# Building the power tables of an RWKV-5 kernel in front of its branch instead of inside it

## The chip, the cores, the metric

The kernel runs on one core of a Trainium2 chip. The metric is the device time of one execution in microseconds; medians of several executions are quoted, with the lowest and highest.

## The reference

A linear-attention block (4 batches, 8 heads, 768 steps, head size 48), then a feed-forward block without a nonlinearity in it.

```python
# attention, per step t; w and u are vectors per head
y[t]  = r[t] @ (state + (u * k[t])^T v[t])
state = w * state + k[t]^T v[t]
# bridge to 3072 x 384, then
a, b = x @ w1, x @ w2
out  = (a * b @ w3) @ w_out
```

The four weights arrive as float64 and are converted on the chip ("pieces" below).

## The kernel before

The 768 steps are cut into 6 chunks of 128; a **unit** is one chunk of one batch, so 24 units, four for each chunk. Inside a unit the decay is handled by tables of powers of w: k is multiplied by rising negative powers and r by falling ones (krs), and then all pairs of steps are one matrix product. The tables are only safe for w in [0.6, 1.6]; a flag computed from w chooses between this first path and a slower one. Everything behind the flag is inside the two arms of a branch.

```python
    # loads of w, unit 0, u, weight piece 0, unit 1, piece 1 are issued here
    nc.vector.tensor_reduce(ends[:, 0:1], wrow, AX.X, ALU.min)
    ...
    inside = nc.values_load(flag[0:1, 0:1], ...)          # the branch reads this

    def body(arm, fast):
        ...
        if fast:
            wn = tab.tile([P, LEVELS + 1, 3 * NP, 1], F32)
            nc.vector.tensor_scalar(wn[:, 0, 0:NP, :], wucol, W_LOW, W_HIGH, ALU.max, ALU.min)
            for l in range(LEVELS):                        # w^2, w^4 ...
                nc.vector.tensor_mul(wn[:, l + 1, 0:NP, :], wn[:, l, 0:NP, :], wn[:, l, 0:NP, :])
            ...                                            # reciprocals, then doubling: both
        for g, t in enumerate(natural):                    # 8 transposes, 2 copies: pn
            ...
        def scale(n):
            kr = krin[n % NIN]
            nc.vector.tensor_mul(krs[n % NS][:, :, :, :D], kr, pn[:, :, :, :D])   # krs
            nc.vector.tensor_mul(ruk, kr[:, 0], kr[:, 1])                         # bonus with u
            nc.vector.tensor_mul(ruk, ruk, ub)
            nc.vector.tensor_reduce(dg, ruk, AX.X, ALU.add)
            # 8 diagonals of AT on ScalarE
        def turn(n):   # krs transposed on TensorE, copied out by ScalarE: kT, rT
        def pairs(n):  # kT x rT on TensorE; VectorE copies the upper triangle into AT
        def output(n): # AT x v on TensorE, copied to xT by ScalarE
        def update(n): # new state: TensorE, then VectorE
        def convert(piece, raw):   # float64 to float32: one pass of ScalarE, six of VectorE
```

Behind this, chunk c's attention runs beside the feed-forward products of chunk c-1 and the conversion of weights. Six pieces (each 128x512; three of w1 and three of w2) must be converted before the first products ps_a and ps_b of the feed-forward part can be finished. The program states what depends on what; the order in each engine's queue is chosen by the scheduler when the kernel is built.

Of the kernel before, what the change touches and what calls it, by code (L numbers as in the profile page):

```python
# [8 lines left out]
F32 = mybir.dt.float32  # L9
# [3 lines left out]
ALU = mybir.AluOpType  # L13
# [3 lines left out]
PSUM = bass.MemoryType.PSUM  # L17
# [3 lines left out]
def kernel(  # L21
# [27 lines left out]
    nc = tc.nc  # L49
    B, H, S, D = r.shape  # L50
    P = 128
    C = 128
    HC = C // 2
    NCH = S // C
    PAD = 64
    NP = H // 2
# [5 lines left out]
    LEVELS = 7  # L62
    PIECE = 512
    W_LOW, W_HIGH = 0.6, 1.6
# [3 lines left out]
    const = ctx.enter_context(tc.tile_pool(name="const", bufs=1))  # L68
# [5 lines left out]
    ident = const.tile([P, P], F32)  # L74
# [13 lines left out]
    wucol = const.tile([P, NP, 1], F32)  # L88
# [46 lines left out]
    for i in range(2):  # L135
# [3 lines left out]
                      in_=u.rearrange("h d -> (h d)").rearrange("(o n) -> o n", o=1).to_broadcast([P, DM]))  # L139
# [8 lines left out]
    nc.vector.tensor_reduce(ends[:, 1:2], wrow, AX.X, ALU.max)  # L148
    nc.vector.tensor_scalar(ends[:, 2:3], ends[:, 0:1], W_LOW, None, ALU.is_ge)
    nc.vector.scalar_tensor_tensor(flag, ends[:, 1:2], W_HIGH, ends[:, 2:3], ALU.is_le, ALU.mult)  # L150
    inside = nc.values_load(flag[0:1, 0:1], min_val=0, max_val=1,
                            skip_runtime_bounds_check_because="a comparison's result is 0 or 1")

    def program(fast):
        with ExitStack() as arm:
            body(arm, fast)

    def body(arm, fast):
        tab = arm.enter_context(tc.tile_pool(name="tab", bufs=1))
        work = arm.enter_context(tc.tile_pool(name="work", bufs=2))  # L160
        psT = arm.enter_context(tc.tile_pool(name="psT", bufs=2, space=PSUM))
# [5 lines left out]
        for t in st:  # L167
            nc.gpsimd.memset(t, 0.0)
        if fast:

            wn = tab.tile([P, LEVELS + 1, 3 * NP, 1], F32)
            nc.vector.tensor_scalar(wn[:, 0, 0:NP, :], wucol, W_LOW, W_HIGH, ALU.max, ALU.min)
            for l in range(LEVELS):
                nc.vector.tensor_mul(wn[:, l + 1, 0:NP, :], wn[:, l, 0:NP, :], wn[:, l, 0:NP, :])  # L174
            nc.vector.reciprocal(wn[:, 0:LEVELS, NP:2 * NP, :], wn[:, 0:LEVELS, 0:NP, :])
            nc.vector.tensor_copy(out=wn[:, 0:LEVELS, 2 * NP:, :], in_=wn[:, 0:LEVELS, 0:NP, :])

            both = tab.tile([P, 2, NP, C], F32)
            nc.vector.memset(both[:, 0, :, HC:HC + 1], 1.0)
            nc.vector.tensor_copy(out=both[:, 1, :, HC:HC + 1], in_=wn[:, 0, NP:2 * NP, :])  # L180
            bf = both.rearrange("x g p t -> x (g p) t")
            for l in range(LEVELS):
                n = 1 << l
                if n < HC:
                    nc.vector.tensor_mul(bf[:, :, HC + n:HC + 2 * n], bf[:, :, HC:HC + n],
                                         wn[:, l, NP:, :].to_broadcast([P, 2 * NP, n]))
                nc.vector.tensor_mul(bf[:, :, HC - 2 * n + 1:HC - n + 1] if n < HC else bf[:, :, 0:1],
                                     bf[:, :, HC - n + 1:HC + 1] if n < HC else bf[:, :, HC:HC + 1],
                                     wn[:, l, 0:2 * NP, :].to_broadcast([P, 2 * NP, n if n < HC else 1]))
            natural = [both[:, g] for g in range(2)]  # L190
        else:
            wn = tab.tile([P, LEVELS + 1, NP, 1], F32)
            nc.vector.tensor_copy(out=wn[:, 0], in_=wucol)
            pw = tab.tile([P, NP, C], F32)
            pr = tab.tile([P, NP, C], F32)
            nc.vector.memset(pw[:, :, 0:1], 1.0)
            nc.vector.memset(pr[:, :, C - 1:C], 1.0)
            for l in range(LEVELS):
                n = 1 << l
                by = wn[:, l].to_broadcast([P, NP, n])  # L200
                nc.vector.tensor_mul(pw[:, :, n:2 * n], pw[:, :, 0:n], by)
                nc.vector.tensor_mul(pr[:, :, C - 2 * n:C - n], pr[:, :, C - n:C], by)
                nc.vector.tensor_mul(wn[:, l + 1], wn[:, l], wn[:, l])
            natural = [pr]
        wc = wn[:, LEVELS, 0:NP, :]
        pn = tab.tile([C, len(natural), H, PAD], F32)
        for g, t in enumerate(natural):
            ps = psT.tile([P, NP, C], F32, tag="t", name=f"ps_p{g}")
            for p in range(NP):
                nc.tensor.transpose(ps[:, p, :], t[:, p, :], ident)  # L210
            nc.scalar.copy(out=pn[:, g].rearrange("t h d -> t (h d)"), in_=ps.rearrange("x p t -> x (p t)"))


        def convert(piece, raw):
# [238 lines left out]
        for c in range(NCH):  # L453
            done = 0
            for b in range(B):
                n = c * B + b
# [52 lines left out]
```

## Time and profile before

| | before |
|---|---|
| time, median of 4 (lowest to highest) | 569.03 us (568.66 to 569.62) |
| span of the profiled execution | 567.8 us |
| TensorE busy / VectorE / ScalarE | 534.4 / 254.9 / 169.2 us |
| VectorE busy in the first 60 us | 46.99 us |
| first transposes of the tables; first krs | 21.46 us; 24.08 us |

How to read the profile: the page's rows of digits cut the span into 40 slices and give an engine's busy share in tenths. The table of stretches gives each engine's busy time (and instructions, in brackets) in a stretch. The timeline lists instructions in order of time: start, duration, engine, line, operation, output <- input, size, count, and in square brackets how long the engine was idle before and what released it. In an engine's list of waits the columns are: who waited, for whom, total us, how many times, the longest. The prediction below shows these lines for the kernel before.

### The profile page before, as it was taken

What the parts mean: (1) busy time and instruction counts of PE and PEld (TensorE: products, weight loads), DVE (VectorE), ACT (ScalarE), POOL (GpSimd) and SP (SyncE); (2) the same over time, 40 slices, a digit from 0 to 9 for tenths busy, and PEclk for the clock granted to TensorE, in tenths of its full rate; (3) what the DMA queues carried; (4) which work ended last, traced back from release to release, by engine and by line L of the source; (5) the groups of instructions that cost most, each with busy time, mean ns of one, the idle gap of its engine ahead of it and who ended that gap; (6) DMA issues with size and microseconds to landing.
All of it is one profiled execution on the core that took longest, in us unless ns stands there. A gap on an engine that the chain in (4) does not pass through costs nothing.

```text
span 567.8 us, 8077 instructions
## 1 busy us (share of the span) xinstructions
PE 534.4 (94%) x3304; PEld 304.8 (54%) x3304; DVE 254.9 (45%) x495; ACT 169.2 (30%) x400; POOL 3.5 (1%) x17
## 2 busy tenths in 40 slices
PE   0388999999999999999999999999999999999996
PEld 0266554555655575566645555655555555544453
DVE  2899999999584596760030404133111100001100
ACT  1555454444333353431121212132132110111010
POOL 2000000000000000000000000000000000000000
PEclk9999999999999999999999999999999999999998
DMA  7675553445233243220120202021010000000001
GB/s 151 171 171 142 132 147 108 128 143 154 43 102 104 87 116 89 66 43 14 43 43 1 65 18 57 15 56 29 16 28 7 9 15 14 29 28 0 0 16 46
DMA packets 84129, 37.52 MB, mean 66 GB/s; under 512 B 76273, under 2 KB 79474, under 8 KB 84082
## 3 DMA queue, kind: packets, MB, share of 16 engines
q1 hardware_dynamic: 84082, 36.91, 25.0%
q8 instruction: 28, 0.46, 0.3%
q14 instruction: 19, 0.16, 0.1%
HBM read 32.18 MB, written 4.72 MB: 65 GB/s over the span
## 4 chain that ended last, share of the span: by engine, by line
PE 87%; DVE 7%; SPq 2%; issue 1%; ACT 1%; DMA 1%; ACTq 0%; DVEq 0%
PE ps_o L406 22%; PE ps_b L400 21%; PE ps_a L395 20%; PE ps_w L259 7%; PE ps_a L299 4%; PE ps_y L355 3%; PE ps_y L347 3%; PE ps_kT L287 2%; PE ps_s L373 2%; PE ps_rT L287 1%; PE ps_w3T L255 1%; SPq L109 1%; DMA krin<-in_r_dram 1%; DVE krs L269 1%; DVE AT L302 1%
## 5 line engine op out<-in xcount | busy, mean ns | idle before, releaser
L401 DVE TENSOR_TENSOR abt<-ps_b,a 128x512 f32<-128x512 f32 x48 | 33.2, 691 | 223.1 <-PE ps_b L400 197.7
L395 PE MATMUL ps_a<-xT,w 128*128 128x512 f32 x288 | 133.2, 597 | 0.0
L400 PE MATMUL ps_b<-xT,w 128*128 128x512 f32 x288 | 132.1, 593 | 0.1
L406 PE MATMUL ps_o<-w,abt 128*128 128x384 f32 x384 | 127.2, 488 | 0.0
L406 PEld LDWEIGHTS ps_o<-w,abt 128*128 128x128 f32 x384 | 72.0, 190 | 49.2 <-issue 2.0
L400 PEld LDWEIGHTS ps_b<-xT,w 128*128 128x128 f32 x288 | 54.4, 190 | 68.9 <-issue 64.3
L395 PEld LDWEIGHTS ps_a<-xT,w 128*128 128x128 f32 x288 | 53.1, 190 | 56.6 <-issue 50.9
L281 ACT ACTIVATE AT<-ident,dg 128x128 f32<-128x128 f32 x192 | 59.1, 391 | 5.8 <-DVE wn L174 3.2
L397 ACT COPY a<-ps_a 128x512 f32<-128x512 f32 x48 | 28.1, 585 | 106.0 <-PE ps_a L395 105.8
L302 DVE COPY_PREDICATED AT<-later,ps_a 128x512 f32<-128x512 int32 x48 | 32.9, 731 | 30.7 <-PE ps_a L299 30.3
L409 ACT COPY osb<-ps_o 128x384 f32<-128x384 f32 x24 | 11.5, 479 | 108.7 <-PE ps_o L406 85.7
L259 PE MATMUL ps_w<-wo,w3T 128*128 128x384 f32 x128 | 43.1, 490 | 0.2 <-ACT w3T L256 0.2
L223 ACT ACTIVATE power<-raw 128x512 f32<-128x512 f32 (+1 forms) x36 | 23.6, 655 | 38.6 <-DVE t L230 23.7
L299 PEld LDWEIGHTS ps_a<-rT,kT 64*128 64x128 f32 x384 | 25.4, 190 | 16.4 <-issue 9.4
L359 ACT COPY xT<-ps_y 128x384 f32<-128x384 f32 x24 | 11.4, 476 | 73.7 <-PE ps_y L355 73.5
L259 PEld LDWEIGHTS ps_w<-wo,w3T 128*128 128x128 f32 x128 | 23.7, 190 | 15.9 <-ACT w3T L256 1.0
L299 PE MATMUL ps_a<-rT,kT 64*128 64x128 f32 x384 | 30.7, 289 | 1.2 <-ACT rT L290 0.8
L355 PE MATMUL ps_y<-AT,vnat 128*32 128x128 f32 x768 | 28.3, 274 | 2.9 <-DVE AT L302 1.5
L290 ACT COPY kT<-ps_kT 128x512 f32<-128x512 f32 x24 | 14.1, 587 | 36.6 <-PE ps_kT L287 36.5
L355 PEld LDWEIGHTS ps_y<-AT,vnat 128*32 128x32 f32 x768 | 22.4, 110 | 4.5 <-DVE AT L302 2.5
L230 DVE SCALAR_TENSOR_TENSOR t<-raw,power 128x512 f32<-128x512 uint32 (+1 forms) x36 | 23.7, 658 | 0.2
L269 DVE TENSOR_TENSOR krs<-krin,pn 128x768 f32<-128x768 f32 x24 | 22.9, 957 | 0.6
(64 smaller groups left out, 335.3 us busy)
## 6 DMA issues: line engine op xcount, KB each, us to landing
raw<-in_moe_w_dram SPq DMA_DIRECT2D x28, 512.0 KB, 3.8
krin<-in_k_dram SPq DMA_DIRECT2D x24, 192.0 KB, 2.7
krin<-in_r_dram SPq DMA_DIRECT2D x24, 192.0 KB, 3.4
vnat<-in_v_dram SPq DMA_DIRECT2D x24, 192.0 KB, 2.8
out_dram<-osb SPq DMA_DIRECT2D x24, 192.0 KB, 1.9
raw<-in_moe_w_out_dram SPq DMA_DIRECT2D x8, 384.0 KB, 3.0
ub<-in_u_dram SPq DMA_DIRECT2D x1, 192.0 KB, 5.3
wucol<-in_w_dram SPq DMA_DIRECT2D x2, 0.8 KB, 1.8
```

The source lines that it names most:

```text
L230: nc.vector.scalar_tensor_tensor(t, lo, 2.0 ** -52, power, ALU.mult, ALU.mult)
L259: nc.tensor.matmul(ps, lhsT=w3T[:, kc, :], rhs=wo[kc], start=(kc == 0), stop=(kc == KF - 1))
L269: nc.vector.tensor_mul(krs[n % NS][:, :, :, :D], kr, pn[:, :, :, :D])
L281: nc.scalar.activation(out=AT[n][:, i, p, :], in_=ident, func=COPY, scale=dg[:, h:h + 1])
L299: nc.tensor.matmul(ps[i][:, p, :], lhsT=kT[n][rows(i), p, :], rhs=rT[n][rows(i), p, :], start=True, stop=True)
L302: nc.vector.copy_predicated(AT[n][:, i], later.bitcast(I32)[:, None, :].to_broadcast([C, NP, C]), ps[i])
L355: nc.tensor.matmul(to(q, g), lhsT=vv[:, p, x:x + Q], rhs=AT[n][:, i, p, :], start=(not c and m < P // Q), stop=True, skip_group_check=True)
L395: nc.tensor.matmul(pa, lhsT=w1[:, q, js], rhs=xT[c][:, q, :], start=(q == 0), stop=(q == KM - 1))
L397: nc.scalar.copy(out=a, in_=pa)
L400: nc.tensor.matmul(pb, lhsT=w2[:, q, js], rhs=xT[c][:, q, :], start=(q == 0), stop=(q == KM - 1))
L401: nc.vector.tensor_mul(abt[c, j], pb, a)
L406: nc.tensor.matmul(po, lhsT=abt[c, j][:, b * C:(b + 1) * C], rhs=w34[:, j, :], start=(j == 0), stop=(j == KF - 1))
```

## The change

The intent: the tables need only w, which lands early, yet in the kernel before their instructions mix in VectorE's queue with work that waits for the first units. Put in front of the branch, they can't be interleaved with anything inside it.

```diff
+    pn_in = const.tile([C, 2, H, PAD], F32)
+    with tc.tile_pool(name="once", bufs=1) as once, tc.tile_pool(name="psW", bufs=2, space=PSUM) as psW:
+        wn_in = const.tile([P, LEVELS + 1, 3 * NP, 1], F32)
+        nc.vector.tensor_scalar(wn_in[:, 0, 0:NP, :], wucol, W_LOW, W_HIGH, ALU.max, ALU.min)
+        ...  # the same squarings, reciprocals and doublings, into wn_in and both
+        for g in range(2):
+            ps = psW.tile([P, NP, C], F32, tag="w", name=f"ps_p{g}")
+            for p in range(NP):
+                nc.tensor.transpose(ps[:, p, :], both[:, g, p, :], ident)
+            nc.scalar.copy(out=pn_in[:, g].rearrange("t h d -> t (h d)"), in_=ps.rearrange("x p t -> x (p t)"))
     inside = nc.values_load(flag[0:1, 0:1], ...)
@@ inside the branch
         if fast:
-            wn = tab.tile(...)   # and all of the above
+            wc, pn = wn_in[:, LEVELS, 0:NP, :], pn_in
```

More of the change, by code (lines that the diff above doesn't have):

```diff
@@ L150 @@
     nc.vector.scalar_tensor_tensor(flag, ends[:, 1:2], W_HIGH, ends[:, 2:3], ALU.is_le, ALU.mult)
+    pn_in = const.tile([C, 2, H, PAD], F32)
+    with tc.tile_pool(name="once", bufs=1) as once, tc.tile_pool(name="psW", bufs=2, space=PSUM) as psW:
+        wn_in = const.tile([P, LEVELS + 1, 3 * NP, 1], F32)
+        nc.vector.tensor_scalar(wn_in[:, 0, 0:NP, :], wucol, W_LOW, W_HIGH, ALU.max, ALU.min)
+        for l in range(LEVELS):
+            nc.vector.tensor_mul(wn_in[:, l + 1, 0:NP, :], wn_in[:, l, 0:NP, :], wn_in[:, l, 0:NP, :])
+        nc.vector.reciprocal(wn_in[:, 0:LEVELS, NP:2 * NP, :], wn_in[:, 0:LEVELS, 0:NP, :])
+        nc.vector.tensor_copy(out=wn_in[:, 0:LEVELS, 2 * NP:, :], in_=wn_in[:, 0:LEVELS, 0:NP, :])
+        both = once.tile([P, 2, NP, C], F32)
+        nc.vector.memset(both[:, 0, :, HC:HC + 1], 1.0)
+        nc.vector.tensor_copy(out=both[:, 1, :, HC:HC + 1], in_=wn_in[:, 0, NP:2 * NP, :])
+        bf = both.rearrange("x g p t -> x (g p) t")
+        for l in range(LEVELS):
+            n = 1 << l
+            if n < HC:
+                nc.vector.tensor_mul(bf[:, :, HC + n:HC + 2 * n], bf[:, :, HC:HC + n],
+                                     wn_in[:, l, NP:, :].to_broadcast([P, 2 * NP, n]))
+            nc.vector.tensor_mul(bf[:, :, HC - 2 * n + 1:HC - n + 1] if n < HC else bf[:, :, 0:1],
+                                 bf[:, :, HC - n + 1:HC + 1] if n < HC else bf[:, :, HC:HC + 1],
+                                 wn_in[:, l, 0:2 * NP, :].to_broadcast([P, 2 * NP, n if n < HC else 1]))
+        for g in range(2):
[3 more added lines that the diff above has]
+            nc.scalar.copy(out=pn_in[:, g].rearrange("t h d -> t (h d)"), in_=ps.rearrange("x p t -> x (p t)"))
     inside = nc.values_load(flag[0:1, 0:1], min_val=0, max_val=1,
@@ L169, in body @@
         if fast:
-            wn = tab.tile([P, LEVELS + 1, 3 * NP, 1], F32)
-            nc.vector.tensor_scalar(wn[:, 0, 0:NP, :], wucol, W_LOW, W_HIGH, ALU.max, ALU.min)
-            for l in range(LEVELS):
-                nc.vector.tensor_mul(wn[:, l + 1, 0:NP, :], wn[:, l, 0:NP, :], wn[:, l, 0:NP, :])
-            nc.vector.reciprocal(wn[:, 0:LEVELS, NP:2 * NP, :], wn[:, 0:LEVELS, 0:NP, :])
-            nc.vector.tensor_copy(out=wn[:, 0:LEVELS, 2 * NP:, :], in_=wn[:, 0:LEVELS, 0:NP, :])
-            both = tab.tile([P, 2, NP, C], F32)
-            nc.vector.memset(both[:, 0, :, HC:HC + 1], 1.0)
-            nc.vector.tensor_copy(out=both[:, 1, :, HC:HC + 1], in_=wn[:, 0, NP:2 * NP, :])
-            bf = both.rearrange("x g p t -> x (g p) t")
-            for l in range(LEVELS):
-                n = 1 << l
-                if n < HC:
-                    nc.vector.tensor_mul(bf[:, :, HC + n:HC + 2 * n], bf[:, :, HC:HC + n],
-                                         wn[:, l, NP:, :].to_broadcast([P, 2 * NP, n]))
-                nc.vector.tensor_mul(bf[:, :, HC - 2 * n + 1:HC - n + 1] if n < HC else bf[:, :, 0:1],
-                                     bf[:, :, HC - n + 1:HC + 1] if n < HC else bf[:, :, HC:HC + 1],
-                                     wn[:, l, 0:2 * NP, :].to_broadcast([P, 2 * NP, n if n < HC else 1]))
-            natural = [both[:, g] for g in range(2)]
+            wc, pn = wn_in[:, LEVELS, 0:NP, :], pn_in
         else:
@@ L203, in body @@
                 nc.vector.tensor_mul(wn[:, l + 1], wn[:, l], wn[:, l])
-            natural = [pr]
-        wc = wn[:, LEVELS, 0:NP, :]
-        pn = tab.tile([C, len(natural), H, PAD], F32)
-        for g, t in enumerate(natural):
-            ps = psT.tile([P, NP, C], F32, tag="t", name=f"ps_p{g}")
+            wc = wn[:, LEVELS]
+            pn = tab.tile([C, 1, H, PAD], F32)
+            ps = psT.tile([P, NP, C], F32, tag="t", name="ps_pr")
             for p in range(NP):
-                nc.tensor.transpose(ps[:, p, :], t[:, p, :], ident)
-            nc.scalar.copy(out=pn[:, g].rearrange("t h d -> t (h d)"), in_=ps.rearrange("x p t -> x (p t)"))
+                nc.tensor.transpose(ps[:, p, :], pr[:, p, :], ident)
+            nc.scalar.copy(out=pn[:, 0].rearrange("t h d -> t (h d)"), in_=ps.rearrange("x p t -> x (p t)"))
         def convert(piece, raw):
```

## The prediction

> **What bounds the kernel now.** I read the page first, then the stretch table, the list of waits by stretch, and the timeline of VectorE for the first 60 us. The page says TensorE, and the last digits of its row say where it does not.
>
> ```profile
> PE 534.4 (94%) x3304; PEld 304.8 (54%) x3304; DVE 254.9 (45%) x495; ACT 169.2 (30%) x400; POOL 3.5 (1%) x17
> PE   0388999999999999999999999999999999999996
> DVE  2899999999584596760030404133111100001100
> ```
>
> A slice is 14.2 us. TensorE is idle in the first slice, a third busy in the second, and full from the fifth. VectorE is the reverse: 45% over the whole, but full from the second to the tenth slice. So the kernel has a head, where VectorE sets the pace, and a long body, where TensorE does. The table of stretches (columns: stretch, its length, busy time and instructions of TensorE, its weight loads, VectorE, ScalarE, GpSimd, then clock, DMA share, GB/s) puts the border near 60 us:
>
> ```profile
> 12.00:18.00 6.00, 0.00 (x0) 0.00 (x0) 4.24 (x17) 2.83 (x11) 0.00 (x0) 1.00 1.04 234
> 18.00:24.00 6.00, 1.94 (x8) 1.57 (x8) 6.00 (x21) 3.69 (x10) 0.00 (x0) 1.00 0.36 111
> 30.00:45.00 15.00, 12.20 (x211) 9.47 (x209) 14.85 (x30) 9.95 (x27) 0.00 (x0) 1.00 0.63 151
> 45.00:60.00 15.00, 13.26 (x175) 9.69 (x176) 14.81 (x28) 7.66 (x21) 0.00 (x0) 1.00 0.64 150
> 60.00:75.00 15.00, 15.00 (x121) 8.17 (x120) 14.82 (x30) 7.81 (x21) 0.00 (x0) 1.00 0.59 157
> ```
>
> From 60 us the list of TensorE's waits shows 0.4 us in all up to the end. An improvement of the head therefore reaches the end nearly whole, and nothing else does. Now the head, from VectorE's timeline (start, duration, engine, line, operation, and in brackets the idle time in front of it and its releaser):
>
> ```profile
> 3.21 0.15 DVE L150 SCALAR_TENSOR_TENSOR flag<-ends 1x1 int32<-1x1 f32 x1
> 4.22 0.28 DVE L172 TENSOR_SCALAR wn<-wucol 128x4 f32<-128x4 f32 x1 [0.86 <-DMA wucol<-in_w_dram]
> 6.24 0.56 DVE L274 TENSOR_TENSOR ruk<-krin 128x384 f32<-128x384 f32 x1 [1.74 <-DMA krin<-in_r_dram]
> 6.72 0.16 DVE L174 TENSOR_TENSOR wn<-wn 128x4 f32<-128x4 f32 x1
> 12.96 0.56 DVE L274 TENSOR_TENSOR ruk<-krin 128x384 f32<-128x384 f32 x1 [6.09 <-DMA krin<-in_r_dram]
> 13.44 0.15 DVE L174 TENSOR_TENSOR wn<-wn 128x4 f32<-128x4 f32 x1
> ...
> 17.89 0.56 DVE L274 TENSOR_TENSOR ruk<-krin 128x384 f32<-128x384 f32 x1 [0.80 <-DMA krin<-in_r_dram]
> ...
> 20.92 0.42 DVE L187 TENSOR_TENSOR both<-both,wn 128x256 f32<-128x256 f32 x1
> ...
> 24.08 1.83 DVE L269 TENSOR_TENSOR krs<-krin,pn 128x768 f32<-128x768 f32 x2
> ```
>
> The order in VectorE's queue mixes the tables (wn, both) with the bonus product ruk of the next units. Its data were on chip at 4.22, but the second squaring stands behind the ruk of unit 1, which waits 6.09 us for a transfer, and the last table stands behind the ruk of unit 2. So TensorE gets the tables at 21.46, pn is in SBUF at 24.05, and the first krs (scaled k and r of unit 0) starts at 24.08. Only then can any pair product run.
>
> [...] GpSimd's first memset behind the branch starts at 4.06, 0.70 us after the flag ends at 3.36. [...] 76273 of 84129 packets are under 512 B, and the engines are 1.04 busy at only 234 GB/s in 12 to 18 us. Hence no krin comes earlier by this change before 18 us.
>
> **The change part by part.** Removed from the branch and put in front of it: 25 VectorE instructions, 8 transposes, 2 ScalarE copies. No arithmetic is added or dropped, no shape changes. The sum of work is the same; what moves is time.
>
> Table time. Interleaved as they are now, the tables' start-to-start distances sum to 3.2 us (first clamp 0.22, memset 0.06, seven squarings 0.07 each, reciprocal 0.24, two copies 0.2, thirteen table products 0.40+0.21+1.34 = 1.95). Alone they run in a dependent chain. The flag's chain shows such a pair: L149 at 3.05, L150 at 3.21, so 0.16 per small step in place of 0.07: seven squarings cost 0.6 more, and about 0.4 more for reciprocal, copy and the first products. So 4.2 us, from 4.22 to **8.4**. From the first transpose to pn it is 24.05 − 21.46 = 2.6 us now; the same behind 8.4 gives pn at **11.1**. That is 13 us earlier than 24.05.
>
> That is not the gain, because VectorE sets the pace of the head and its work stays. From 24 to 135 us its list of waits has one entry, 0.9 us. What can be won is idle time of VectorE. Now it idles 0.87+1.17+0.86+1.74+6.09+0.80+0.91 = **12.4 us** up to 28.3. After the change I count: 0.87+1.17+0.86 as before (nothing lands sooner); 1.0 latency inside the chain of tables; 0.7 for its branch, now behind the tables, which takes it to 9.1; ruk of unit 0 to 9.6. Then the order decides. If the ruk of unit 1 still stands in front of the first krs, 12.96 − 9.6 = 3.3 idle; together 7.9. If krs of unit 0 comes first, about 2.0 from 9.1 to 11.1; together 6.6. Behind that there is enough to do up to the landing of unit 2 at 17.89: two krs 1.8, the ruk and dg of two units 2.8, the first converted weight piece 3.1, AT of unit 0 1.3, together 9.0 against 4.9 to 6.8 us. So the gain is 12.4 − 7.9 = 4.5 or 12.4 − 6.6 = 5.8, less a lost 0 to 1 for a wait on ScalarE or a raw piece. I choose 5.0, and 568.8 − 5.0 = **563.8 us**.
>
> **The rivals.**
> (1) The whole 13 us come through, 556 us. For it: TensorE's first real work, krs, is the last link before all else, and 13 us is what its input gains. Against it: VectorE is at 14.85 of 15 in 30 to 45 us, and the first two-weight product of the second part, ps_b at 59.85, comes with the sixth converted piece (its last addition ends at about 60). It can't come earlier than VectorE's work allows.
> (2) A transfer takes the place of the wait, gain 0 to 2 us, 567 to 569. For it: DMA is full from 4.5 to 18 us, so units 1 and 2 land at 12.96 and 17.89 whatever VectorE does, and an earlier VectorE runs into them. Against it: its share is 0.36 in 18 to 24 and 0.63 later, and the loads that follow wait for buffers that VectorE would free sooner (the krin load at 25.07 starts as the first krs ends).
> (3) The order of the whole branch is laid out anew, since its start differs; a few us either way, at TensorE's border above all. Neither trace nor source shows its size.
> (4) ScalarE or TensorE becomes late because each now passes its branch only behind the tables (about 11 us). Against it: raw of piece 0 lands at 11.41 and TensorE has nothing before krs. I give it under 1 us.
>
> **Range and chances.** Rival 2 gives the upper end, 567.5; a good order with half of rival 1 the lower end, 558.5. Faster by over 2% needs 557.4, a gain of 11.4 of the 12.4 us that VectorE idles, hence 0.06. Slower by over 2% would need 11.4 us of new waits in a body that has none: 0.01. The rest, 0.93, is within 2%.
>
> **What would show it.** In the changed kernel: last table product at about 8.4 and first transpose just behind it; pn at about 11; first krs at 11 to 15; VectorE's idle time up to 28 us at 7 to 8 instead of 12.4; VectorE near full from 18 us on; TensorE without waits from about 55 us instead of 60; busy sums of all engines unchanged within 1%. I am wrong if the order puts krs behind the ruk of unit 2 again (krs after 18 us), if TensorE's waits between 60 us and the end grow past 2 us, or if VectorE turns out not to pace the head, so that the gain follows krs.

Sentences of the prediction on the hardware in general, which no trace of this case shows, are cut, and the cuts are marked. Its sum came to 568.8 − 5.0 = 563.8 us, and the 0.7 us for the branch is taken from the trace (the flag ends at 3.36, GpSimd's first memset starts at 4.06). What it calls a full DMA from 4.5 to 18 us is a mean share of 0.96 in the table of stretches.

## The result

| | before | after |
|---|---|---|
| time, median of 4 | 569.03 us | 565.00 us (564.53 to 565.27) |
| span of the profiled execution | 567.8 us | 562.7 us |
| mean granted clock of TensorE | 0.997 | 0.989 |
| VectorE busy in the first 60 us | 46.99 us | 51.54 us |
| first transposes of the tables; first krs | 21.46; 24.08 us | 8.00; 10.65 us |

The ratio is 0.9927 (95% interval 0.991 to 0.9945). Ratios here are the mean time of one kernel's fast runs over that of the other's of the same rounds, so not quite the ratio of the medians. The change is clearly real and clearly under 2%.

The rows of digits of the changed kernel, for TensorE, VectorE and the granted clock:

```profile
PE   3869999999999999999999999999999999999996
DVE  5999999998674696840220414233211100001100
PEclk9969999999999999999999999999999999999999
```

VectorE is full one slice sooner and done sooner. TensorE starts earlier but is no better in its third slice (6), and its clock falls there, which it did not before. VectorE's timeline of the changed kernel, same columns as in the prediction:

```profile
3.57 0.17 DVE L157 TENSOR_SCALAR wn_in<-wucol 128x4 f32<-128x4 f32 x1 [0.22 <-DMA wucol<-in_w_dram]
...
3.78 1.34 DVE L159 TENSOR_TENSOR wn_in<-wn_in 128x4 f32<-128x4 f32 x7
...
7.43 0.42 DVE L172 TENSOR_TENSOR both<-both,wn_in 128x256 f32<-128x256 f32 x1
10.65 0.96 DVE L277 TENSOR_TENSOR krs<-krin,pn_in 128x768 f32<-128x768 f32 x1 [2.80 <-ACT pn_in L179]
...
12.57 0.96 DVE L277 TENSOR_TENSOR krs<-krin,pn_in 128x768 f32<-128x768 f32 x1 [0.50 <-DMA krin<-in_r_dram]
...
17.45 0.56 DVE L282 TENSOR_TENSOR ruk<-krin 128x384 f32<-128x384 f32 x1 [0.65 <-DMA krin<-in_r_dram]
17.92 1.34 DVE L310 COPY_PREDICATED AT<-later,ps_a 128x512 f32<-128x512 int32 x2
```

The squarings now run back to back, 1.34 us for seven. The tables end at 7.85, and VectorE waits 2.80 us for pn. The first krs stands in front of the products of unit 1 and starts 13.43 us earlier than before. AT of unit 0 is made at 17.92, before at 29.75: 11.8 us earlier. And yet the end came only 4 to 5 us earlier. Where the other 8 us went can be followed unit by unit: the second half of AT ends at 31.1, 34.3, 41.7, 46.3, 55.6, 62.9 us for units 0 to 5 before, and at 19.3, 25.4, 30.0, 41.6, 50.4, 58.6 after. The lead is 11.8, 8.9, 11.7, and from unit 3 on 4.7, 5.2, 4.3 us.

What ends the lead at unit 3 are two things beside VectorE. First, ScalarE's queue in the changed kernel has the eight diagonals between its two copies of unit 3 (its timeline):

```profile
34.62 0.59 ACT L298 COPY kT<-ps_kT 128x512 f32<-128x512 f32 x1 [2.45 <-PE ps_kT L295]
35.10 2.45 ACT L289 ACTIVATE AT<-ident,dg 128x128 f32<-128x128 f32 x8
37.45 0.56 ACT L298 COPY rT<-ps_rT 128x512 f32<-128x512 f32 x1
```

so TensorE waits 2.7 us for rT. Second, TensorE's clock. The table of stretches for three short stretches of the changed kernel (the number behind GpSimd's brackets is the granted clock):

```profile
28.00:30.00 2.00, 0.79 (x13) 0.40 (x11) 2.00 (x5) 1.35 (x4) 0.00 (x0) 1.00 0.38 75
30.00:32.00 2.00, 1.42 (x34) 1.15 (x36) 1.94 (x5) 0.88 (x2) 0.00 (x0) 0.87 0.37 83
34.00:36.00 2.00, 1.38 (x7) 0.98 (x5) 1.91 (x6) 1.38 (x5) 0.00 (x0) 0.50 1.05 196
```

After 2.2 us of work in 4 us, with idle times of 1.02, 0.19 and 0.58 us between, the clock was 0.50 from 32 to 41 us (0.65 from 41 to 42, then 1.00). In the same rows VectorE is busy 2.00, 1.94 and 1.91 of 2 us. That is the question for the experiments: did the stall at unit 3 and the half clock eat the lead (**theory B**), or was it never there to be had, because VectorE had no time to use it (**theory A**, that of the prediction)?

### The profile page after: what moved, and what is told of

The parts are those of the page before. It is cut to its first block, busy times and chain, and to the rows that moved or that the text cites. A ratio compares the mean times of both kernels' runs of the same rounds, so it can differ in the third digit from the quotient of the medians.

```text
span 562.7 us, 8088 instructions
## 1 busy us (share of the span) xinstructions
PE 539.0 (96%) x3304; PEld 307.2 (55%) x3304; DVE 255.5 (45%) x495; ACT 169.2 (30%) x400; POOL 3.6 (1%) x17
## 4 chain that ended last, share of the span: by engine, by line
PE 90%; DVE 6%; DMA 1%; issue 1%; ACT 1%; SPq 0%; DVEq 0%; ACTq 0%
PE ps_o L414 22%; PE ps_b L408 22%; PE ps_a L403 22%; PE ps_w L267 7%; PE ps_a L307 5%; PE ps_y L363 4%; PE ps_y L355 3%; PE ps_kT L295 2%; PE ps_s L381 2%; PE ps_rT L295 2%; PE ps_w3T L263 1%; DVE t L238 1%; DVE AT L310 1%; DMA raw<-in_moe_w_dram 1%; DVE w L239 1%
## 5 line engine op out<-in xcount | busy, mean ns | idle before, releaser
L277 DVE TENSOR_TENSOR krs<-krin,pn_in 128x768 f32<-128x768 f32 x24 | 22.9, 956 | 3.8 <-ACT pn_in L179 2.8
```

## The experiments

Twelve kernels were run, in three groups, each group on one chip with the kernel before beside it. They are told in the order of the argument, so 12 and 11 stand before 10. Times are medians; "against after" compares with 565.00 us, and ratios with 0.9927.

**1. The tables stay inside the branch, but go first.** Every later instruction of VectorE in the branch was queued behind the tables:

```diff
 kernel before, inside body()
-                nc.vector.tensor_mul(bf[...], bf[...], wn[...])
+                last = nc.vector.tensor_mul(bf[...], bf[...], wn[...])
...
+        queue.enter_context(tc.issue_after(last.ins))     # around all units
         scale(0)
```

> The kernel before, with the tables left inside the branch, but every other instruction of VectorE in the branch queued behind the squarings and copies of the tables. Theory A (VectorE paces the head, the gain is the idle time it loses): the tables end near 9 us, VectorE then waits for unit 1 until about 12.9 us, and its idle time up to 30 us falls from 12.4 to about 7 us; time about 564 us, as good as the change, although the first krs comes at about 16 us, 5 us later than in the changed kernel. Theory B (the moment of the first krs sets the gain): krs at 16 us is 8 us earlier than before against 13.4 us in the changed kernel, so the gain is about 60% of 4.0 us, about 566.5 us. Theory C (the place in front of the branch is what counts): no gain, 569 us.

Measured: 563.87 us (563.51 to 564.49), ratio 0.9906 (0.9891 to 0.992). VectorE's timeline of this kernel:

```profile
4.34 0.28 DVE L172 TENSOR_SCALAR wn<-wucol 128x4 f32<-128x4 f32 x1 [0.86 <-DVE flag L150]
...
9.99 0.56 DVE L276 TENSOR_TENSOR ruk<-ruk,ub 128x384 f32<-128x384 f32 x1 [2.34 <-DMA ub<-in_u_dram]
...
15.84 1.82 DVE L270 TENSOR_TENSOR krs<-krin,pn 128x768 f32<-128x768 f32 x2
```

The edge had been hung on the last product in program order, which depends on little and runs early, so ruk of unit 0 still slipped into the tables and met a wait of 2.34 us for u. The first krs came at 15.84, 5.2 us later than in the changed kernel. The time was as good all the same, and so was VectorE's idle time up to 28 us: 6.5 us, against 6.75 in the changed kernel. (The clock stayed at 0.996 to 0.999 here, against 0.989; experiment 9 comes back to what that is worth.) So the moment of krs does not set the gain (against B's 566.5), and the place in front of the branch is not needed for it (against C's 569): the order is.

**2 and 3. Spare work for VectorE behind the tables, in front of the branch.** Three and ten products of 128x512 that nobody reads; the order in the branch stays that of the changed kernel (compared for the first hundred instructions of VectorE).

```diff
 changed kernel, behind the tables
+        for _ in range(3):                                # or 10
+            nc.vector.tensor_mul(spare, both[:, 0], both[:, 1])
```

> The changed kernel with three products of 128x512 (about 1.8 us of VectorE) put behind the last table product in front of the branch, read by nobody. They fall into the 2.8 us in which VectorE waits for pn. Theory A: nothing is lost, 565 us within 0.6. If instead all added work of VectorE costs its full length: 566.8 us.

> The changed kernel with ten such products (about 6.0 us of VectorE), same order in the branch. 2.1 to 2.8 us of it lie in the wait for pn, the rest delays VectorE. Theory A: the rest, 3.2 to 3.9 us, comes out at the end one for one: about 568.5 us. Theory B (latency of the units through TensorE and ScalarE limits): krs moves from 10.65 to about 14 us, and since 13.4 us of krs gave 4.0 us, 3.5 us of krs give about 1 us: 566 us.

Measured: with three, 565.08 us (563.95 to 567.57), ratio 0.9927 (0.9909 to 0.9945), the same as the changed kernel. With ten, 568.20 us (567.21 to 568.34), ratio 0.9973 (0.996 to 0.9986). VectorE's timeline with ten:

```profile
7.89 7.23 DVE L177 TENSOR_TENSOR spare<-both 128x512 f32<-128x512 f32 x10
15.32 0.96 DVE L280 TENSOR_TENSOR krs<-krin,pn_in 128x768 f32<-128x768 f32 x1 [0.20 <-DMA raw<-in_moe_w_dram]
```

They cost 0.72 us each, not the 0.6 I had taken (in the kernel before, a 128x512 product starts at 22.32 and the next instruction at 22.93), so 7.2 us in all; 2.8 lie in the wait for pn, and krs comes 4.67 us later. The time grew by 3.2 us, not by the 4.4 that are left: the changed kernel's two waits for transfers, 0.50 and 0.65 us, are gone in this run, which makes up the difference. The expected 568.5 was met although the size of a product behind it was not. Here krs is at 15.32, about where experiment 1 has it (15.84), and the times differ by 4.3 us. The same first krs, another time: what differs is how much of VectorE's time before it was work. Theory A holds for both; B, which gives the two the same time, falls.

**4. The bonus products of units 0 to 5 on GpSimd.**

```diff
-            nc.vector.tensor_mul(ruk, kr[:, 0], kr[:, 1])
-            nc.vector.tensor_mul(ruk, ruk, ub)
+            eng = nc.gpsimd if n < 6 else nc.vector
+            eng.tensor_mul(ruk, kr[:, 0], kr[:, 1])
+            eng.tensor_mul(ruk, ruk, ub)
```

> The changed kernel with the two products for the bonus (ruk) of units 0 to 5 on GpSimd in place of VectorE, which takes 6 x 0.94 = 5.6 us of work off VectorE in the head. Theory A: VectorE reaches the border about 5 us earlier and the end follows, about 560 us, provided that GpSimd keeps up and the two don't slow each other. Theory B (ScalarE's late copy of rT for unit 3 and the low clock of TensorE there set the end): within 1 us of 565 us.

Measured: 570.59 us (569.25 to 571.07), ratio 1.0016 (1.0003 to 1.0029): both theories missed. GpSimd and VectorE did slow each other. The timelines of VectorE and of GpSimd in this kernel:

```profile
13.36 1.49 DVE L232 SCALAR_TENSOR_TENSOR w<-power,raw 128x512 f32<-128x512 f32 x1
14.88 1.10 DVE L234 TENSOR_SCALAR t<-w 128x512 uint32<-128x512 uint32 x1
...
17.31 0.68 DVE L232 SCALAR_TENSOR_TENSOR w<-power,raw 128x512 f32<-128x512 f32 x1
```

```profile
12.52 1.78 POOL L283 TENSOR_TENSOR ruk<-krin 128x384 f32<-128x384 f32 x1 [1.48 <-DMA krin<-in_r_dram]
14.26 2.57 POOL L284 TENSOR_TENSOR ruk<-ruk,ub 128x384 f32<-128x384 f32 x2
```

The same conversion step took 1.49 us while GpSimd worked and 0.68 us after it had stopped; the plain bitwise step 1.10 against 0.41. GpSimd's first product for a unit took 1.78 us at 12.52, beside VectorE's krs, and 1.00 us at 23.61. Not every instruction was slowed: the reduction dg took its usual 0.53 us at 28.37, beside a product on GpSimd. The run does not test A, since VectorE got no time back (126.35 us of work up to 135 us, against 125.80 in the changed kernel, with twelve products fewer). Nor is this slowing alone to blame: the order changed as well, the first reductions dg came at 22.98 instead of 14.39, and AT of unit 0 at 27.14 instead of 17.92.

**5. The stall at unit 3 taken away.** ScalarE copies rT before it makes the diagonals, units 0 to 5.

```diff
-            # diagonals of AT in scale(n)
+            # ... in turn(n), queued behind the copy of rT
+                with tc.issue_after(copied.ins):
+                    diagonals(n, owed.pop(n))
```

> The changed kernel with ScalarE's copy of rT queued ahead of the eight diagonals of the same unit, for units 0 to 5; this takes away TensorE's wait of 2.7 us for rT of unit 3 and should spare it the low clock between 31 and 41 us. Work of VectorE the same. Theory A (VectorE paces the head): within 1 us of 565. Theory B (that wait and the low clock ate most of the 13 us): 3 to 5 us faster, about 561.

Measured: 564.61 us (563.76 to 564.71), ratio 0.9915 (0.9901 to 0.9928). The wait for rT fell from 2.7 to 0.8 us, and the time did not follow. But TensorE did not stop waiting; it now stands in front of ps_y of unit 3:

```profile
38.23 1.33 DVE L321 COPY_PREDICATED AT<-later,ps_a 128x512 f32<-128x512 int32 x2
39.05 0.64 PE L374 MATMUL ps_y<-AT,vnat 128*32 128x128 f32 x4 [3.97 <-issue]
```

VectorE, busy without a gap from 35.19 us on, came to AT of unit 3 only at 38.23; the profile names no releaser, but TensorE goes on as the first half of AT ends (about 38.9). TensorE's waits behind the tables add to 10.4 us up to 60 us, against 10.0 in the changed kernel. So the stall was moved rather than taken away, from ScalarE's copy to VectorE's; that speaks for A, and the first half of theory B falls. The clock still fell (0.78 from 30 to 45 us, 0.992 on the mean), so the other half stays for experiment 9.

**6. Less work for VectorE.** No product with u for units 0 to 5, no last addition for the first six pieces; relative error 0.31. Its output is wrong, which doesn't matter for the time.

```diff
+            if n >= 6:
                 nc.vector.tensor_mul(ruk, ruk, ub)
...
+            if not any(src is p[1] for p in ab_pieces[:6]):
                 nc.vector.tensor_add(dst, dst, t)
```

> The changed kernel with less work for VectorE in the head and nothing put in its place: no product with u for units 0 to 5 (6 x 0.47 us) and no last addition for the first six weight pieces (6 x 0.6 us), 6.4 us in all. The result is wrong on purpose. Theory A: up to 6.4 us faster, about 559; less where VectorE then runs into transfers or into TensorE. Theory B: no more than 1 us faster.

Measured: 560.99 us (558.91 to 561.82), ratio 0.9849 (0.9829 to 0.9868): 4.0 us of 6.4 against after. More than B allows, less than one for one. VectorE's waits for ps_a and for a krin grew from 0.7 and 0.6 to 1.5 and 1.4 us, but in all it idled only 1.1 us more of the first 60 us (9.6 against 8.5). That leaves about 1.3 us of the missing 2.4 unexplained. With 6 us less to do, VectorE seems no longer alone in setting the pace.

**7. The first states on ScalarE.**

```diff
-                    nc.vector.tensor_mul(own, ps[rows(i), :, 0:D], wc[rows(i)].to_broadcast([PAD, NP, D]))
+                    for p in range(NP):
+                        nc.scalar.activation(out=own[:, p, :], in_=ps[rows(i), p, 0:D], func=COPY, scale=wc[rows(i), p, :])
```

> The changed kernel with the first state of each batch (two products of 0.35 us each, four units) written by ScalarE, eight small scaled copies a unit, in place of VectorE; correct. VectorE loses 2.8 us of work in the head, ScalarE, which is half idle there, gains some 6 us. Theory A: 1.5 to 3 us faster than 565, about 562.5. Theory B (ScalarE's queue limits): slower than 565.

Measured: 561.47 us (559.47 to 563.03), ratio 0.9862 (0.9841 to 0.9884), correct: 3.5 us against after, the fastest correct kernel. More than the 2.8 us of work moved (ScalarE's eight copies took 1.73 to 1.75 us a unit, 7.0 in all where some 6 were expected), and its runs scatter by 3.6 us. Its clock was 0.995 to 1.0, against 0.989 in the changed kernel, so a part may be the clock's. Experiments 10 and 11 show that the size does not carry over.

**8. Spare work for VectorE behind the border**, twelve products of 128x384 at units 8 and 9.

```diff
+            if n in (8, 9):
+                for _ in range(6):
+                    nc.vector.tensor_mul(ruk, kr[:, 0], kr[:, 1])
```

> The changed kernel with twelve more products of 128x384 on VectorE for units 8 and 9, 5.6 us of work at about 95 to 110 us, where VectorE is still full but TensorE has no waits. If TensorE sets the pace from about 60 us on: within 1 us of 565. If VectorE, being full up to 135 us, paces that stretch too: about 570.

Measured: 566.32 us (565.59 to 567.90), ratio 0.9944 (0.993 to 0.9957): 1.3 us against after (the intervals overlap), not the 5.6. The products ran from 90.7 to 105.4 us; from 90 to 105 us VectorE was busy 14.86 of 15 us. TensorE's waits behind 60 us stayed at 0.9 us. So VectorE may be full without setting the pace; from 60 us on it has a backlog that TensorE does not wait for. Even the 1.3 us need not come from them: in the profiled run, the slowest of the five at 567.90 us, the clock had already fallen to half at 20 us, in a head whose order is that of the changed kernel.

```profile
20.00:24.00 4.00, 4.00 (x52) 3.08 (x50) 1.93 (x5) 1.81 (x5) 0.00 (x0) 0.50 0.78 208
```

In that stretch VectorE worked 1.93 of 4 us, against 3.43 in the changed kernel. It waited 2.1 us for TensorE there, for ps_s; a second wait for ps_s at 49 us brings this to 3.2 us.

**9. Spare transposes that hold the clock**, 64 of them, in TensorE's gaps between 23 and 47 us.

```diff
+        def filler(n, k, behind):                         # behind update(n) and turn(n), units 0 to 3
+            with tc.issue_after(behind.ins):
+                ps = psF.tile([P, KF // 2, P], F32, tag="f", ...)
+                for q in range(k):
+                    nc.tensor.transpose(ps[:, q % (KF // 2), :], ident, ident)
```

> The changed kernel with spare transposes on TensorE (8 to 20 of 128x128 per unit, 60 in all, into a bank that nothing reads) in its gaps between 20 and 45 us, so that its clock is not lowered there. VectorE's work is the same. If VectorE alone paces the head: within 1 us of 565. If the half clock from 31 to 41 us cost part of the gain: 2 to 3 us faster, about 562.5, and with less scatter between runs.

Measured: 563.83 us (563.26 to 565.63), ratio 0.991 (0.9895 to 0.9925). The recorded clock held (0.996 to 1.0 in all five runs). The medians differ by 1.2 us, and the interval overlaps that of the changed kernel. So from 23 us on, the low clock did not eat the 8 us of lead. What it cost in all stays open, because the spare transposes start only at 23.0 us. Before them TensorE came late in this profiled run (the slowest of the five), although the table of stretches gives a clock of 1.00 from 12 to 30 us: from the start of AT of unit 0 to that of the state which needs ps_s there were 4.77 us (18.37 to 23.14), in the changed kernel 3.13 (17.92 to 21.05), and VectorE waited for ps_s:

```profile
23.14 0.82 DVE L399 TENSOR_TENSOR st<-ps_s,wn_in 64x192 f32<-64x192 f32 x2 [2.07 <-PE ps_s L390]
```

So a late TensorE acts through VectorE's waits, here (2.07 us) and in experiment 8 (2.1 us). Among the kernels with the changed order the two slowest runs, 567.57 us in experiment 2 and 567.90 us in experiment 8, are the two with the lowest clock, 0.981, while their siblings at 0.989 to 0.993 took 563.95 to 566.37 us. The prediction of less scatter did not hold (2.4 us).

**12. The wait for pn filled with work that has to be done anyway**: piece 0 is loaded first and converted behind the tables, in front of the branch.

```diff
-    load(0)
-    ...
-    landed = {0: fetch(ab_pieces[0])}
+    landed = {0: fetch(ab_pieces[0])}
+    load(0)
...
+        nc.scalar.activation(out=power0, in_=hi.bitcast(F32), func=ABS)
+        with tc.issue_after(table.ins):
+            ...   # the six VectorE passes of convert() for piece 0
```

> The changed kernel with the first weight piece loaded ahead of unit 0 and converted in front of the branch behind the tables, so that VectorE works (3.3 us) while TensorE and ScalarE make pn, where it waited 2.8 us. No work is added or dropped. Theory A: the wait of 2.8 us goes, the first krs comes about 1 us later (11.8), the time falls by about 2 us to 563. Theory B (latency of the first units): about 1 us slower than 565.

Measured: 562.83 us (561.74 to 563.66), ratio 0.9888 (0.9871 to 0.9905), correct: 2.2 us faster than after, as A said, with the first krs 1.1 us later (the six passes ran from 7.76 to 11.54, 3.8 us where 3.3 were expected):

```profile
10.85 0.69 DVE L187 TENSOR_TENSOR w<-w,t 128x512 f32<-128x512 f32 x1
11.75 0.96 DVE L290 TENSOR_TENSOR krs<-krin,pn_in 128x768 f32<-128x768 f32 x1 [0.20 <-DVE w L187]
```

The size is partly luck. The 2.80 us are gone, but new waits for TensorE, 1.8 and 1.1 us, took most of that back: VectorE idled 5.8 us up to 28 us, against 6.75. The rest came from 30 to 60 us (0.4 us idle against 1.3), where the clock was less low (0.89 from 30 to 45 us, against 0.66); on the mean it was 0.996 to 0.999, and experiment 9, with such a clock and nothing moved, is only 1.0 us slower than this one, with overlapping intervals. The direction is plain, together with experiment 3: useful work in the gap did not lengthen the kernel, useless work beyond the gap did, and krs is delayed by both.

**11. The first states on ScalarE, in the kernel before.** The edit is that of experiment 7.

> The kernel before with the first states on ScalarE (2.8 us less for VectorE in the head), as in the run of the changed kernel where this brought 3.5 us. Theory A: the same here, 2 to 3.5 us faster than before, about 566.

Measured: 569.53 us (568.99 to 570.67), ratio 1.0012 (0.9998 to 1.0026): nothing, against theory A. The table of stretches suggests why:

```profile
30.00:45.00 15.00, 12.94 (x197) 9.76 (x198) 13.76 (x26) 12.73 (x42) 0.00 (x0) 0.89 0.63 151
45.00:60.00 15.00, 13.07 (x190) 9.44 (x188) 14.59 (x28) 14.88 (x50) 0.00 (x0) 1.00 0.70 162
```

ScalarE is busy 14.88 of 15 us from 45 to 60, and VectorE is no longer full from 30 to 45. The states of units 0 to 3 (1.75 us of ScalarE each) fall together with the diagonals, the copies and the conversions there; in the changed kernel the same work came from 21 to 39 us, and ScalarE had 6.26 of 15 us to do from 45 to 60. So it looks as if VectorE's time can be cashed in only where ScalarE has room; no run tests this.

**10. All that had helped, together**: experiments 7, 9 and 12.

> All that theory A says should help, put together: the changed kernel, the first piece converted in the wait for pn (2 us), the first states on ScalarE (3 us), spare transposes that keep the clock (0 to 2 us): 558 to 560 us, correct.

Measured: 563.13 us (562.22 to 563.70), ratio 0.9892 (0.9877 to 0.9908), correct. No better than experiment 12 alone. VectorE was busy 53.92 us of the first 60, as wanted, but the first product of the feed-forward part came at 50.77 us, in experiment 12 at 43.38. TensorE was busy 14.42 of 15 us from 30 to 45, so it had few gaps left for the spare transposes; I take it that these now cost what they saved, but no run without them was made, and the loss stays open.

## Why the prediction was right

It said 563.8 us (558.5 to 567.5), within 2%; measured 565.00.

**That VectorE paces the head: shown, within limits.** Two lines of the table of stretches, for the first 60 us, of the kernel before and of the changed one:

```profile
0.00:60.00 60.00, 32.22 (x423) 24.87 (x424) 46.99 (x110) 28.46 (x73) 3.54 (x17) 1.00 0.67 157
```

```profile
0.00:60.00 60.00, 41.92 (x458) 29.44 (x458) 51.54 (x118) 30.84 (x78) 3.58 (x17) 0.91 0.72 169
```

VectorE got 4.55 us more done in the first 60 us, and the span shrank by 5.1 us. TensorE's busy time there grew by 9.7 us, part of it at half clock, and bought nothing more. The same count for every kernel that has the same work to do before the border (spare products taken off, span of the same execution):

| kernel | VectorE's useful work in 60 us | span | sum |
|---|---|---|---|
| before | 46.99 | 567.8 | 614.8 |
| 3, ten spare products | 54.86 − 7.23 = 47.63 | 566.5 | 614.1 |
| 8, late spare products | 48.05 | 566.1 | 614.2 |
| 9, spare transposes | 50.41 | 563.8 | 614.2 |
| 2, three spare products | 52.67 − 2.14 = 50.53 | 563.7 | 614.2 |
| after | 51.54 | 562.7 | 614.2 |
| 5, rT first | 51.75 | 562.6 | 614.4 |
| 1, order only | 52.66 | 561.7 | 614.4 |
| 12, piece 0 in the gap | 53.38 | 561.2 | 614.6 |

Work gained and span lost agree within 0.5 us about their mean. This table alone says only how far VectorE had come by 60 us, not who held it up: in row 8 it was behind because it waited for TensorE. That its free time is the cause rests on the runs in which that time was changed on purpose: 3 and 6 above all, with 1, 2 and 12. The limits are experiment 11, where 2.8 us less work brought nothing, and the clock, whose share, by my estimate 1 us or more (experiment 9 held it and was 1.2 us faster), no run isolates. Where work was moved off VectorE or left out (4, 6, 7, 10, 11) this account does not hold, because another engine's time comes in or, in 4, the slowing of VectorE beside GpSimd.

**The cost of the tables: right.** Predicted 4.2 us from the clamp; measured 3.57 to 7.85, 4.3 us. **pn at 11.1:** measured 10.56, earlier because the clamp was. I had counted 0.86 us of idle time in front of it as a wait for w that would stay. It was 0.22: w had landed by 3.57, and the 0.86 us in the kernel before was the branch itself, as experiment 1 shows, where the same 0.86 us is put down to the flag.

**The branch at 0.7 us: too dear.** In the changed kernel it lies inside the wait for pn. Where it is exposed, in experiments 3 and 12, VectorE is idle 0.20 us.

**VectorE's idle time:** 12.4 us before; predicted 6.6 if krs of unit 0 comes first, which it did. Measured up to 28 us: 0.87+1.29+0.22+2.80+0.50+0.65+0.42 = 6.75 us. That the sums agree so closely is partly luck. The 0.86 came as 0.22; the 1.0 inside the tables is no idle time in the profile; 0.7 and 2.0 came together as 2.80. In their place stand 0.50+0.65+0.42 = 1.57 us of waits for two transfers and for TensorE, which the prediction had held to be covered: "there is enough to do up to the landing of unit 2". There was, but it stood in the queue behind the ruk of unit 2: the rest of the first piece ran at 19.14. **The 0 to 1 us lost later:** from 30 to 60 us VectorE idled 15.00−14.19+15.00−14.55 = 1.26 us, of which 0.65 in front of AT of unit 3; before, 0.34. The 0.65 follows from the late copy of rT and the half clock, which the prediction did not foresee. VectorE's account is thus 12.4 − 6.75 = 5.7, less 0.9, so 4.8 us; the medians fell by 4.0.

**Rival 1, the whole 13 us:** refuted by experiments 1 and 3. **Rival 2, transfers:** small, 0.50 and 0.65 us; units 1 and 2 were used at 12.57 and 17.45, 0.4 us sooner than before. **Rival 3, a new order:** it did come, and put krs first; its own effect was not measured apart. **Rival 4, ScalarE late behind its branch:** no; its first work inside starts at 10.89, as the raw piece lands. **TensorE's border:** predicted at 55 us instead of 60; it came sooner, as TensorE has no wait from 46 us to the end except 0.7 us at 84.9 and 0.2 us. **Busy sums** within 1%: VectorE 255.5 against 254.9, ScalarE unchanged, TensorE 539.0 against 534.4, 0.9% more, in line with the clock (0.989 on the mean against 0.997).

## What to carry to other kernels

Where a result that all else waits for becomes ready 13 us sooner, ask which engine must then do the work that follows, and count that engine's idle time up to the point where another takes over: that, not the lead, is what the gain followed here (VectorE's idle time up to 28 us fell by 5.7 us, the lead was 13.4, the gain 4.0). An engine that is full is not always the one that sets the pace (in experiment 8 VectorE was busy 14.86 of 15 us, and twelve more products there went with 1.3 us, where 5.6 were added); put spare work into it and see whether the end moves. Work whose data are ready should not stand in an engine's queue behind work that waits for a transfer (here the second squaring stood behind a wait of 6.09 us), and an edge in the scheduler's graph avoids that as well as another place in the program (563.87 us in experiment 1, 565.00 with the change).
